# Second factor of a two-stage Fourier mixing: cosine and sine products in sixteen 32x32 tiles, two steps at a time

## The chip, the cores and the metric

The kernel runs on one core of a Trainium2 chip. The metric is the device time of one execution in microseconds (us). The median of three runs before the change is 2624.26 us (2623.59 to 2626.94).

## What is computed

Two blocks follow one another, all in fp32:

```python
# block 1: 8 sequences of 3008 rows, 256 channels; a filter in the frequency domain
X = np.fft.rfft(x, axis=1)                       # x: (8, 3008, 256)
Y = X * (filt_r + 1j * filt_i)[None, :, :]       # 1505 frequencies
y = np.fft.irfft(Y, n=3008, axis=1)
# block 2: every row through an ELU network
h = y.reshape(24064, 256) @ w_in                 # w_in: (256, 2048)
g = np.where(h > 0, h, np.exp(np.minimum(h, 0)) - 1)
out = g @ w_out                                  # w_out: (2048, 256)
```

## The kernel before, in words

**Block 1** is a Fourier transform in two factors, 3008 = 47 x 64. For each sequence ("batch" b) six `a_unit`s apply the factor of 64 and write to DRAM (`z_write`); eight steps g apply the factor of 47 and the filter (`b_unit`), four `bi_unit`s take the inverse factor of 47 (two steps at once) and write to DRAM (`y_write`), and six `n_unit`s (L438) take the inverse factor of 64. `b_unit` (L372) is what the change replaces. It has 16 matmuls whose weights are 48 rows by 32 columns: the 24 cosine and 24 sine rows of a table lie above each other, so that one matmul forms cosine product plus (or, for the other column half c, minus) sine product by itself. Real parts go to the PSUM tile `psr`, imaginary parts to `psi`. Then VectorE (DVE) multiplies both by the filter `f` (`products`, L328, four operations of 128x512 on a PSUM and an SBUF operand), and GpSimd (POOL) forms six sums in SBUF (L388 to L393; three small copies more in step 0).

**Block 2** takes the rows in 192 "items": 8 batches x 6 units m x 4 quarters q, each a multiplication by a quarter of `w_in` in Strassen-Winograd form: seven up steps (`up_steps`, L474; two matmuls each, for the trace four records, as each fp32 matmul is recorded twice), the ELU, and seven down steps by a quarter of `w_out` (`down_steps`, L559), one item later. In the prediction, U1 to U7 and D1 to D7 are these steps by the number of their product. The up steps run in the order U1 U2 U6 U5 U7 U3 U4, the down steps in the order D1 D3 D5 D7 D6 D2 D4. What matters of the up steps:

```python
def s2(): add("b11", mm(2, "a", True), g["t1"]); done("a")        # L517, DVE L497 from PSUM pha
def s7(): add("b22", mm(7, "d", True), g["t4"]); elu_max("b11", g["b11"])   # bank phd, DVE L497
def s3(): p = mm(3, "s", False); elu_exp("b12", p); ...; elu_max("b12", p); done("s")
def s4(): add("b21", mm(4, "d", False), g["t2"]); done("d"); elu_max("b22", g["b22"])
```

After U4, `tail` (L544) issues `elu_exp` of b21 and five DVE operations (L547, L548, L511, L550, L551). U4 accumulates into the same PSUM bank (`phd`) that U7 wrote, so its matmuls have to wait until DVE has read U7's result: the sum b22 of `s7`. `elu_exp` is two operations on ScalarE (ACT, L506 and L507), `elu_max` one on DVE (L511); `keep` (L500) is a copy by ACT.

**PSUM.** Four banks are dealt out in turn by the list `banks` (L187): each `bank()` takes the first, and its number is put back at the end of the list where the program is done with it. A `b_unit` takes two, a `bi_unit` all four.

**The order** is written by hand. The program runs over "quads", one per item (L903 to L922). In each quad the up steps of item i and the down steps of item i - 1 are interleaved by a string; between its first and second half come the planned units of place 0, at its end those of place 1:

```python
for k in "DUUDUDDU" if i in opens else "UUDUDDU": ...     # first half
for fn, a in plan.get((i, 0), ()): fn(*a)                 # place 0
for k in "DUUDUD" if i in opens else "DUUDUDD": ...       # second half
if up_tail: up_tail()
if down_tail: down_tail()
for fn, a in plan.get((i, 1), ()): fn(*a)                 # place 1
```

A quad in `opens` starts with a down step, which gives the banks time to come free. The plan repeats every 24 quads (one batch; "quad 10" below is the tenth of the 24). Seven batches have the steps of block 1 in it; the first has them ahead of the loop. Before, `b_unit`s stand at place 1 of quads 9, 10, 12, 13, 15, 16, 18, 19, `bi_unit`s at place 1 of 11, 14, 17, 20; quads 12, 15, 18, 21 open. Others in the plan: `x_unit` (L213, DVE), `c_unit` (four DVE sums, L587, place 0 of quads 1, 5, 9, 13, 17, 21), `o_unit` (two DVE transposes, L609, place 0 of 2, 6, 10, 14, 18, 22), three DVE sums of `down_steps`' tail (L587, at the end of quads 0, 4, 8, 12, 16, 20), `n_unit` and its three DVE sums `n_sums` (L458). Every engine takes its instructions in program order.

Of the kernel before, what the change touches and what calls it, by code (L numbers as in the profile page):

```python
# [14 lines left out]
ALU = mybir.AluOpType  # L15
# [26 lines left out]
def _make_tables():  # L42
# [58 lines left out]
    fb, bb = np.zeros((P, 2, 2, 32)), np.zeros((P, 2, 4, 32))  # L101
    for r in (LO, HI):
        fb[r, :, 0, :24] = gb[r, :, 0:24]
        fb[r, 0, 1, 1:24] = gb[r, 0, 24:47]
        fb[r, 1, 1, :24] = gb[r, 1, 24:48]
# [6 lines left out]
    pairs = np.concatenate([fb.reshape(P, P), bb.reshape(P, 2 * P)], 1)  # L112
# [18 lines left out]
def kernel(  # L131
# [27 lines left out]
    qp = pool("qp", 1)  # L159
    t3p = pool("t3p", 1)  # L160
# [8 lines left out]
    pairs = glob.tile([P, 3 * P], FP32, name="pairs")  # L169
    fb = pairs[:, 0:P].rearrange("p (v c k) -> p v c k", v=2, c=2)  # L170
    bb = pairs[:, P:3 * P].rearrange("p (v a i) -> p v a i", v=2, a=4)
# [71 lines left out]
    def x_place_first(c):  # L243
        if c < XBUFS:
            t = xp.tile([P, 2, 2, D], FP32, tag="xc", name="xc").rearrange("p k u d -> p (k u) d")
        else:
            t = t1p.tile([P, XC, D], FP32, tag="t1", name="x1")
        if c < 2:
            w = tnp.tile([P, 4, P], FP32, tag="tn", name="tn")
# [57 lines left out]
    def z_read(b, g):  # L307
        t = t2s[b, g] = t2p.tile([P, 4, D], FP32, tag="t2", name="t2")
        for p, r in enumerate((0, 24, 64, 88)):
            k = p * K2 + 4 * g  # L310
            nc.sync.dma_start(t[r:r + 24].rearrange("i u d -> i (u d)"), zs[b][:, k:k + 4, :].rearrange("i u d -> i (u d)"))
# [60 lines left out]
    def b_unit(b, g):  # L372
        t = t2s.pop((b, g))
        f = fbufs[(b * NG + g) % FBUFS]
        (i0, re), (i1, im) = (bank(n) for n in ("psr", "psi"))
        for c in range(2):
            for a in range(4):
                for ps, k in ((re, LO), (im, HI)):
                    nc.tensor.matmul(ps[32 * a:32 * a + 32, c, :], fb[k, 1 if g == a == 0 else 0, c, :], t[k, a, :],  # L379
                                     start=True, stop=True)  # L380
        sr, si = (sp.tile([P, 2, D], FP32, tag=n, name=n) for n in ("sr", "si"))
        if g % 2 == 0:
            ss[b, g] = qp.tile([P, 4, 2, D], FP32, tag="z", name="zs")
        z = ss[b, g - g % 2][:, :, g % 2]
        p, q = z[:, 0:2], z[:, 2:4]
        products(re, im, f, sr, si, p, q)
        banks.extend((i0, i1))
# [14 lines left out]
    def bi_unit(b, g):  # L402
        z = ss.pop((b, g))
# [302 lines left out]
    def f_arrange():  # L706

        for c, src in enumerate((filt_r, filt_i)):
            for a in range(2):
                nc.gpsimd.dma_start(fd[:, a, 0:48:2, c, :, :].rearrange("g q u d -> q g (u d)"),  # L710
                                    raw(src, 2 * a, [[64 * D, 24], [4 * D, NG], [1, 2 * D]]))
                for u in range(2):
                    g0 = 1 if a == u == 0 else 0
                    for j, n in ((0, 16), (16, 7)):
# [20 lines left out]
    with tc.manual_schedule():  # L735


        with tc.tile_pool(name="boot", bufs=1) as bp:
# [131 lines left out]
        for b in range(B):  # L870
            t = (b - 1) * PER
            if b > 0:
                for c, s in enumerate((2, 2, 4, 4, 7, 7)):
                    at(t + s, 0, x_unit, b, c)
                    if c % 2 == 0:
                        opens.add(t + s + 1)
                        at(t + s, 1, a_unit, b, c)
                    nb, nxt = (b, c + XBUFS) if c + XBUFS < NXC else (b + 1, c + XBUFS - NXC)
                    if nb < B:
                        at(t + s, 1, x_load, nb, nxt)  # L880
                    at(t + s, 1, z_write, b, c)
                for g in range(NG):
                    s = t + 9 + g + g // 2
                    at(s, 1, b_unit, b, g)
                    at(s - 2, 1, f_read, b, g)
                    at(s - 2, 1, z_read, b, g)
                    if g % 2:

                        opens.add(s + 2)
                        at(s + 1, 1, bi_unit, b, g - 1)  # L890
                        at(s + 1, 1, y_write, b, g - 1)
            for m, (s, place) in enumerate(((23, 0), (25, 1), (29, 1), (32, 0), (36, 0), (40, 0))):
                if b > 0 or m > 0:
# [4 lines left out]
                    at(*((t + s + 1, 1) if m == 5 else (t + s, place)), n_sums, b, m)  # L898
# [56 lines left out]
```

## Time and profile before

| | |
|---|---|
| median of three runs | 2624.26 us |
| the profiled execution, its own time | 2626.73 us |
| its span in the trace | 2624.9 us |
| busy: PE, DVE, ACT, POOL | 2556.2, 1891.1, 1483.2, 488.0 us |
| matmuls of b_unit (L379), psr and psi | 896 + 896 records, 376 ns each |
| DVE, L330 to L333 (products, 56 each) | 0.68 us each |
| POOL L388 | 56, mean 1.27 us |

PE is TensorE's matmuls. A row of the profile's groups reads: line, engine, operation, what is written <- what is read, shapes, count | busy time, mean of one | idle time of the engine just before it, and what ended that idle time. A row of the timeline reads: start, duration, engine, line, operation, operands, count. Successive operations of an engine overlap a little in the records (a DVE operation of 0.68 us is followed by the next one 0.60 us after its start), and full-array matmul records of 0.38 us start 0.216 us apart.

### The profile page before, as it was taken

To read this page: it belongs to the slowest core of one execution; us is meant where nothing else is said; L and a number is where in the kernel's file an instruction comes from. 1 tells how busy PE (TensorE), PEld (TensorE's weight loads), DVE (VectorE), ACT (ScalarE), POOL (GpSimd) and SP (SyncE) were. 2 spreads that over 40 slices of the span, in tenths; PEclk is the share of its full clock that TensorE was granted. 3 is DMA by queue.
4 is the path that set the end of the run, shared out by engine and by line. 5 is a ranking of instruction groups with operands and counts; after the bars stand their busy time and mean duration, and the time that the engine had idled before them with its cause. 6 is when DMAs were issued, how large, how long until landed. Compare 5 with 4: busy or idle time off the path is not lost.

```text
span 2624.9 us, 45659 instructions
## 1 busy us (share of the span) xinstructions
PE 2556.2 (97%) x17604; PEld 2173.1 (83%) x17604; DVE 1891.1 (72%) x3251; ACT 1483.2 (57%) x2574; POOL 488.0 (19%) x669
## 2 busy tenths in 40 slices
PE   5799999999999999999999999999999999999998
PEld 4588788888898888988889888888788888898887
DVE  6886777678777777777767777677777768766766
ACT  6565555555555555655555555555555555555554
POOL 5102330024200331004310133002340023300000
PEclk8899999999999999999999999999999999999999
DMA  9633221432224232232314231143321332210010
GB/s 275 185 102 101 72 61 36 121 87 59 67 66 113 61 87 48 66 102 66 88 41 102 73 99 48 41 106 87 91 56 40 84 82 63 61 37 18 19 27 17
DMA packets 227449, 200.50 MB, mean 76 GB/s; under 512 B 129554, under 2 KB 199410, under 8 KB 227232
## 3 DMA queue, kind: packets, MB, share of 16 engines
q1 hardware_dynamic: 209928, 160.60, 24.6%
q0 software_dynamic: 15856, 36.25, 4.9%
q8 instruction: 139, 2.28, 0.4%
q10 hardware_dynamic: 1448, 0.72, 0.1%
q14 instruction: 78, 0.64, 0.1%
HBM read 125.62 MB, written 78.17 MB: 78 GB/s over the span
## 4 chain that ended last, share of the span: by engine, by line
PE 91%; DVE 3%; ACT 2%; issue 0%; DMA 0%; SPq 0%; ACTq 0%; DVEq 0%
PE po L571 42%; PE phs L489 25%; PE phd L489 12%; PE pha L489 6%; PE psr L379 2%; PE psa L230 2%; PE pv L412 1%; DVE y L454 1%; PE psn L447 1%; DVE g L497 1%; ACT e L506 1%; ACT e L507 1%; ACT g L500 1%; ACT ys L452 0%; DVE ys L465 0%
## 5 line engine op out<-in xcount | busy, mean ns | idle before, releaser
L571 PE MATMUL po<-g,wo 128*128 128x256 f32 (+1 forms) x5376 | 1308.6, 376 | 0.0
L571 PEld LDWEIGHTS po<-g,wo 128*128 128x128 f32 x5376 | 1014.2, 190 | 142.7 <-issue 20.0
L500 ACT ACTIVATE g<-phs 128x512 f32<-128x512 f32 (+1 forms) x576 | 339.4, 589 | 827.6 <-PE phs L489 827.6
L497 DVE TENSOR_TENSOR g<-phd,g 128x512 f32<-128x512 f32 (+1 forms) x384 | 259.6, 676 | 376.9 <-ACT e L507 318.5
L507 ACT ACTIVATE e<-e 128x512 f32<-128x512 f32 (+1 forms) x768 | 477.4, 622 | 24.4
L511 DVE SCALAR_TENSOR_TENSOR g<-e,g 128x512 f32<-128x512 f32 (+1 forms) x576 | 400.5, 695 | 2.5 <-ACT e L507 1.3
L489 PE MATMUL phs<-y,wi 128*128 128x256 f32 (+1 forms) x1536 | 396.3, 380 | 1.4 <-DVE y L454 1.4
L489 PE MATMUL phs<-ys,wi 128*128 128x256 f32 (+1 forms) x1536 | 388.3, 375 | 1.5 <-ACT g L500 1.5
L506 ACT ACTIVATE e<-g 128x512 f32<-128x512 f32 (+1 forms) x576 | 353.7, 614 | 51.6 <-DVE g L511 24.3
L489 PEld LDWEIGHTS phs<-y,wi 128*128 128x128 f32 x1536 | 284.3, 190 | 58.1 <-issue 11.5
L489 PEld LDWEIGHTS phs<-ys,wi 128*128 128x128 f32 x1536 | 292.1, 190 | 35.6 <-ACT g L500 2.4
L388 POOL TENSOR_TENSOR sr<-sr,zs 128x512 f32<-128x512 f32 x56 | 71.3, 1273 | 1130.6 <-DVE zs L332 1130.6
L489 PE MATMUL phd<-ys,wi 128*128 128x256 f32 (+1 forms) x768 | 197.5, 380 | 16.4 <-DVE g L497 16.4
L511 DVE SCALAR_TENSOR_TENSOR g<-e,phs 128x512 f32<-128x512 f32 (+1 forms) x192 | 129.7, 675 | 110.4 <-ACT e L507 110.4
L506 ACT ACTIVATE e<-phs 128x512 f32<-128x512 f32 (+1 forms) x192 | 113.0, 589 | 146.8 <-PE phs L489 146.8
L489 PE MATMUL pha<-y,wi 128*128 128x256 f32 (+1 forms) x768 | 194.4, 376 | 0.0
L489 PE MATMUL phd<-y,wi 128*128 128x256 f32 (+1 forms) x768 | 193.7, 375 | 0.0
L489 PEld LDWEIGHTS phd<-ys,wi 128*128 128x128 f32 x768 | 142.8, 190 | 45.4 <-DVE g L497 30.5
L454 DVE SCALAR_TENSOR_TENSOR y<-ys,psn 128x512 f32<-128x512 f32 (+1 forms) x96 | 60.4, 671 | 148.5 <-ACT ys L452 148.5
L489 PEld LDWEIGHTS pha<-y,wi 128*128 128x128 f32 x768 | 146.4, 191 | 16.7
L489 PEld LDWEIGHTS phd<-y,wi 128*128 128x128 f32 x768 | 145.8, 190 | 16.5
L497 DVE TENSOR_TENSOR g<-pha,g 128x512 f32<-128x512 f32 (+1 forms) x192 | 129.1, 673 | 40.0 <-PE pha L489 40.0
(129 smaller groups left out, 2367.5 us busy)
## 6 DMA issues: line engine op xcount, KB each, us to landing
t<-yd SPq DMA_DIRECT2D x95, 256.0 KB
z<-t SPq DMA_DIRECT2D x84, 256.0 KB
f<-fp POOLq DMA_DIRECT2D x224, 96.0 KB, 3.0
t<-z SPq DMA_DIRECT2D x224, 96.0 KB
yd<-t SPq DMA_DIRECT2D x112, 192.0 KB
out_dram<-o SPq DMA_DIRECT2D x632, 32.0 KB
xc<-in_x_dram SPq DMA_DIRECT2D x84, 128.0 KB
xc<-in_x_dram SPq DMA_DIRECT2D x161, 64.0 KB
```

The lines of the kernel that those rows point to most:

```text
L230: nc.tensor.matmul(p[o:o + 64, u, :], w[r, u, o:o + 64], src[r, u, :], start=True, stop=True)
L379: nc.tensor.matmul(ps[32 * a:32 * a + 32, c, :], fb[k, 1 if g == a == 0 else 0, c, :], t[k, a, :], start=True, stop=True)
L388: nc.gpsimd.tensor_tensor(out=sr, in0=sr, in1=p, op=ALU.add)
L412: nc.tensor.matmul(pv[a][1][32 * p:32 * p + 32, js, :], bb[r, v, p, :], z[r, p, js, :], start=True, stop=True, tile_position=(32 * a, 32 * p))
L454: nc.vector.scalar_tensor_tensor(out=y, in0=s[:, 0:2], scalar=v, in1=even[:, :, 0:h], op0=ALU.mult, op1=ALU.add)
L489: nc.tensor.matmul(ps[:, a, 0:h], w_in[q][:, COMBO[n], a, :], y[n], start=start and a == 0, stop=True, skip_group_check=True)
L497: nc.vector.tensor_tensor(out=g[o], in0=i0, in1=i1, op=ALU.add)
L500: nc.scalar.activation(out=g[o], in_=i0, func=AXT.Copy)
L506: nc.scalar.activation(out=e, in_=src, func=AXT.Relu, scale=-1.0)
L507: nc.scalar.activation(out=e, in_=e, func=AXT.Exp, scale=-1.0)
L511: nc.vector.scalar_tensor_tensor(out=g[n], in0=es[n], scalar=1.0, in1=src, op0=ALU.subtract, op1=ALU.max)
L571: nc.tensor.matmul(po[i][:, u, 0:h], w_out[q][:, COMBO[n], a, :], g[n][:, a, :], start=q == 0 and a == 0 and n in (1, 3, 6, 4), stop=True, ...
```

## The change

`b_unit` is split into `b_pair` (two steps g and g + 1 at once) and `b_products` (one step).

`b_pair` has 32 matmuls with weights of 24 rows by 32 columns: cosine and sine products are apart, each in one of four row groups (`tile_position`), and go to four PSUM banks (xr, yr, yi, xi). ACT copies yr and yi to SBUF; DVE then forms sum and difference of x and y for real and imaginary parts (four operations of 128x512), into the SBUF tiles `s` (a new pool) and `z`; in step 0 four copies of 32x256 follow. `b_products` multiplies as before, but reads SBUF alone and works in place; then POOL does what it did. `b_pair` and the products of the even step stand at place 1 of quads 9, 12, 15, 18, the products of the odd step at place 0 of the next quad; `bi_unit` stays where it was. Quads 10, 13, 16 and 19 open now, besides 12, 15, 18, 21. Reads of the filter and of z for both steps are issued together, two quads ahead of `b_pair`. `n_unit` of m = 4 moves from place 0 of quad 12 to place 0 of 14, that of m = 5 from place 0 to place 1 of 16, and every `n_sums` half a quad later. The table `fb` is cut to 64 columns, the padding of the filter is written as zeros, and some tiles of the start come from other pools.

```diff
+    for p, (r, c) in enumerate(((0, 0), (24, 24), (64, 24), (88, 0))):
+        fb[32 * p:32 * p + 24, 0, :24] = gb[r:r + 24, 0, 0:24]
+        fb[32 * p:32 * p + 24, 1, :24] = gb[r:r + 24, 1, c:c + 24]
...
-        for p, r in enumerate((0, 24, 64, 88)):
+        for p in range(4):
             k = p * K2 + 4 * g
-            nc.sync.dma_start(t[r:r + 24].rearrange("i u d -> i (u d)"), zs[b][:, k:k + 4, :].rearrange("i u d -> i (u d)"))
+            nc.sync.dma_start(t[32 * p:32 * p + 24].rearrange("i u d -> i (u d)"), zs[b][:, k:k + 4, :].rearrange("i u d -> i (u d)"))
...
-    def b_unit(b, g):
-        t = t2s.pop((b, g))
+    def b_pair(b, g):
+        t = [t2s.pop((b, g + j)) for j in range(2)]
+        pb = [bank("psb") for _ in range(4)]
+        for j in range(2):
+            for a in range(4):
+                for p, (_, ps) in enumerate(pb):
+                    r = slice(32 * p, 32 * p + 24)
+                    nc.tensor.matmul(ps[32 * a:32 * a + 32, j, :], fb[r, 1 if g == j == a == 0 else 0, :], t[j][r, a, :],
+                                     start=True, stop=True, tile_position=(32 * p, 32 * a))
+        s = rp.tile([P, 2, 2, D], FP32, tag="s", name="s")
+        z = qp.tile([P, 4, 2, D], FP32, tag="z", name="zs")
+        ss[b, g] = s, z
+        xr, yr, yi, xi = (ps for _, ps in pb)
+        ur, ui = (sp.tile([P, 2, D], FP32, tag=n, name=n) for n in ("sr", "si"))
+        nc.scalar.activation(out=ur, in_=yr, func=AXT.Copy)
+        nc.scalar.activation(out=ui, in_=yi, func=AXT.Copy)
+        for o, x, u in ((s, xr, ur), (z, xi, ui)):
+            nc.vector.tensor_tensor(out=o[:, 0], in0=x, in1=u, op=ALU.add)
+            nc.vector.tensor_tensor(out=o[:, 1], in0=x, in1=u, op=ALU.subtract)
+        if g == 0:
+            for o, x, u in ((s, xr, ur), (z, xi, ui)):
+                nc.vector.tensor_copy(out=o[0:32, 0, 0], in_=x[0:32, 0])
+                nc.vector.tensor_copy(out=o[0:32, 1, 0], in_=u[0:32, 0])
+        banks.extend(pb[p][0] for p in (1, 2, 0, 3))
+
+    def b_products(b, g):
         f = fbufs[(b * NG + g) % FBUFS]
-        (i0, re), (i1, im) = (bank(n) for n in ("psr", "psi"))
-        for c in range(2):
-            for a in range(4):
-                for ps, k in ((re, LO), (im, HI)):
-                    nc.tensor.matmul(ps[32 * a:32 * a + 32, c, :], fb[k, 1 if g == a == 0 else 0, c, :], t[k, a, :],
-                                     start=True, stop=True)
...
-        products(re, im, f, sr, si, p, q)
-        banks.extend((i0, i1))
+        s, z = ss[b, g - g % 2]
+        sr, p, q = s[:, :, g % 2], z[:, 0:2, g % 2], z[:, 2:4, g % 2]
+        n = "sr" if g % 2 else "si"
+        si = sp.tile([P, 2, D], FP32, tag=n, name=n)
+        nc.vector.tensor_tensor(out=si, in0=sr, in1=f[:, 1], op=ALU.mult)
+        nc.vector.tensor_tensor(out=sr, in0=sr, in1=f[:, 0], op=ALU.mult)
+        nc.vector.tensor_tensor(out=q, in0=p, in1=f[:, 0], op=ALU.mult)
+        nc.vector.scalar_tensor_tensor(out=p, in0=p, scalar=-1.0, in1=f[:, 1], op0=ALU.mult, op1=ALU.mult)
         nc.gpsimd.tensor_tensor(out=sr, in0=sr, in1=p, op=ALU.add)
...
-                for g in range(NG):
+                for g in range(0, NG, 2):
                     s = t + 9 + g + g // 2
-                    at(s, 1, b_unit, b, g)
-                    at(s - 2, 1, f_read, b, g)
-                    at(s - 2, 1, z_read, b, g)
-                    if g % 2:
-                        opens.add(s + 2)
-                        at(s + 1, 1, bi_unit, b, g - 1)
-                        at(s + 1, 1, y_write, b, g - 1)
-            for m, (s, place) in enumerate(((23, 0), (25, 1), (29, 1), (32, 0), (36, 0), (40, 0))):
+                    opens.update((s + 1, s + 3))
+                    at(s, 1, b_pair, b, g)
+                    for j in range(2):
+                        at(s - 2, 1, f_read, b, g + j)
+                        at(s - 2, 1, z_read, b, g + j)
+                        at(s + j, 1 - j, b_products, b, g + j)
+                    at(s + 2, 1, bi_unit, b, g)
+                    at(s + 2, 1, y_write, b, g)
+            for m, (s, place) in enumerate(((23, 0), (25, 1), (29, 1), (32, 0), (38, 0), (40, 1))):
...
-                    at(*((t + s + 1, 1) if m == 5 else (t + s, place)), n_sums, b, m)
+                    at(t + s + place, 1 - place, n_sums, b, m)
```

More of the change, by code (lines that the diff above doesn't have):

```diff
@@ L97, in _make_tables @@
     gi[0:24, 1, 24:48], gi[24:48, 1, 0:24] = -m0 * s0.T, -m3 * s3.T
[L101 to L105, printed above, removed]
+    fb, bb = np.zeros((P, 2, 32)), np.zeros((P, 2, 4, 32))
+    for p, (r, c) in enumerate(((0, 0), (24, 24), (64, 24), (88, 0))):
+        fb[32 * p:32 * p + 24, 0, :24] = gb[r:r + 24, 0, 0:24]
+        fb[32 * p:32 * p + 24, 1, :24] = gb[r:r + 24, 1, c:c + 24]
     for o in range(0, P, 32):
@@ L111, in _make_tables @@
     bb[0:24, 1, 2, :24], bb[0:24, 1, 3, :24] = gi[24:48, 1, 0:24], gi[0:24, 1, 24:48]
-    pairs = np.concatenate([fb.reshape(P, P), bb.reshape(P, 2 * P)], 1)
+    pairs = np.concatenate([fb.reshape(P, 64), bb.reshape(P, 2 * P)], 1)
     lie = np.concatenate([2 * np.arange(24), 2 * np.arange(24) + 1])
@@ L146 @@
     ]
+    none_d = nc.inline_tensor(np.zeros((NG, 2 * D), np.float32), name="none_t").ap()
     def pool(name, bufs, **kw):
@@ L159 @@
     qp = pool("qp", 1)
+    rp = pool("rp", 1)
     t3p = pool("t3p", 1)
@@ L167 @@
     psM = pool("psM", 1, space=PSUM)
-    pairs = glob.tile([P, 3 * P], FP32, name="pairs")
-    fb = pairs[:, 0:P].rearrange("p (v c k) -> p v c k", v=2, c=2)
-    bb = pairs[:, P:3 * P].rearrange("p (v a i) -> p v a i", v=2, a=4)
+    pairs = glob.tile([P, 64 + 2 * P], FP32, name="pairs")
+    fb = pairs[:, 0:64].rearrange("p (v k) -> p v k", v=2)
+    bb = pairs[:, 64:].rearrange("p (v a i) -> p v a i", v=2, a=4)
     w_in, w_out = ([glob.tile([P, 7, 2, P], FP32, name="%s%d" % (n, i)) for i in range(4)] for n in ("wi", "wo"))
@@ L248, in x_place_first @@
         if c < 2:
-            w = tnp.tile([P, 4, P], FP32, tag="tn", name="tn")
+            w = sp.tile([P, 4, P], FP32, tag="s" + "ri"[c], name="tf")
         else:
@@ L367, in y_write_first @@
             queues[p // 2].dma_start(yds[0][32 * p + 4 * g:32 * p + 4 * g + 4].rearrange("u i d -> i u d"), t[r:r + 24])
-    def b_unit(b, g):
-        t = t2s.pop((b, g))
-        f = fbufs[(b * NG + g) % FBUFS]
-        (i0, re), (i1, im) = (bank(n) for n in ("psr", "psi"))
-        for c in range(2):
-            for a in range(4):
-                for ps, k in ((re, LO), (im, HI)):
-                    nc.tensor.matmul(ps[32 * a:32 * a + 32, c, :], fb[k, 1 if g == a == 0 else 0, c, :], t[k, a, :],
-                                     start=True, stop=True)
[L381 to L385, printed above, removed]
-        products(re, im, f, sr, si, p, q)
-        banks.extend((i0, i1))
+    def b_pair(b, g):
[22 more added lines that the diff above has]
+        banks.extend(pb[p][0] for p in (1, 2, 0, 3))
@@ L402, in bi_unit @@
     def bi_unit(b, g):
-        z = ss.pop((b, g))
+        _, z = ss.pop((b, g))
         t = t3s[b, g] = t3p.tile([P, 2, 4, D], FP32, tag="t3", name="t3")
@@ L719, in f_arrange @@
                 g0 = 0 if a else 1
-                nc.gpsimd.dma_start(fd[g0:NG, a, 47, c, :, :].rearrange("g u d -> g (u d)"),
-                                    raw(src, 4, [[2 * D, NG - g0], [1, 2 * D]]))
+                nc.gpsimd.dma_start(fd[g0:NG, a, 47, c, :, :].rearrange("g u d -> g (u d)"), none_d[g0:NG])
             nc.gpsimd.dma_start(fd[0, 0, 1:48:2, c, 0, :], raw(src, 32, [[64 * D, 24], [1, D]]))
-            nc.gpsimd.dma_start(fd[0, 0, 47:48, c, 1, :], raw(src, 4, [[D, 1], [1, D]]))
+            nc.gpsimd.dma_start(fd[0, 0, 47:48, c, 1, :], none_d[0:1, 0:D])
     def f_pairs(c, u):
@@ L744 @@
             zq = qp.tile([P, 4, 2, D], FP32, tag="z", name="zq")
-            pqs = [[(sp if i == 0 else bp).tile([P, 2, D], FP32, name="s%s" % n, **({"tag": "s" + n} if i == 0 else {}))
-                    for n in "ri"] +
-                   [zq[:, 0:2, i], zq[:, 2:4, i]] for i in range(2)]
             t3f = t3p.tile([P, 2, 4, D], FP32, tag="t3", name="t3")
@@ L807 @@
             w_join(6)
+            pqs = [[(sp if i == 0 else bp).tile([P, 2, D], FP32, name="s%s" % n, **({"tag": "s" + n} if i == 0 else {}))
+                    for n in "ri"] +
+                   [zq[:, 0:2, i], zq[:, 2:4, i]] for i in range(2)]
             for g in range(4):
```

## The prediction

> **What bounds the kernel now.** I read the page's busy times and the chain that ended last, then PE's list of waits, then the timeline around one batch's steps.
>
> ```profile
> PE 2556.2 (97%) x17604; PEld 2173.1 (83%) x17604; DVE 1891.1 (72%) x3251; ACT 1483.2 (57%) x2574; POOL 488.0 (19%) x669
> ...
> PE 91%; DVE 3%; ACT 2%; issue 0%; DMA 0%; SPq 0%; ACTq 0%; DVEq 0%
> ```
>
> PE is the bound: it idles 69 us, most of it in the first 120 us. PE's time is what counts, and whatever makes PE wait. In the loop only one wait recurs:
>
> ```profile
> PE phd L489 <- DVE g L497: 16.4, 29, 0.7
> ```
>
> This is U4 waiting for DVE's sum b22 (front section). U7's end leaves DVE two steps of PE, 1.73 us, to do it. The timeline shows it at 1163.66 in quad 8, behind the `n_unit`'s five DVE operations, and U4 0.66 us late. So DVE has 28% to spare on average and none at this place: what is queued ahead of b22 shows as a stall of PE. The change queues more there.
>
> **PE's saving.** The unit of 16 matmuls (32 records) before: the D step ahead of it starts at 1260.01, its last record is at 1260.66; the unit's records run from 1260.97 to 1261.69; U1 starts at 1261.99, with its second record 0.32 later instead of 0.216. Added to PE: 1261.99 - 1260.66 - 0.216 = 1.117, plus 0.104 = 1.22 us. For sixteen tiles of 32x32 the nearest row is `bi_unit`:
>
> ```profile
> 1011.69 0.59 PE L571 MATMUL po<-g,wo 128*128 128x256 f32 x2
> 1012.22 1.14 PE L412 MATMUL pv<-zs,pairs 24*32 24x512 f32 x32
> 1013.29 0.70 PE L571 MATMUL po<-g,wo 128*128 128x256 f32 x2
> ```
>
> Its 32 records are twice as wide as b_pair's and need 1.07 us to the next step, two rounds of sixteen, 0.45 us apart; sixteen tiles do run at once. b_pair has four rounds of 256 columns: 0.31 (lead) + 0.77 (0.24 + 2 x 0.215 to the fourth round, then 15 issues at 0.0067) + 0.31 - 0.216 + 0.104 = 1.27 us. A pair saves 2 x 1.22 - 1.27 = 1.17 us, 28 pairs **-32.7 us**. If only eight tiles ran at once, it were four more rounds of 0.215, and -8.6 us in all.
>
> **What DVE gets.** Let T be b_pair's first record. The records of b_pair end 0.77 after T, D1 starts at 1.08; in an opening quad twelve steps of 0.864 us stand ahead of U4, so U4 is due at 1.08 + 0.10 + 12 x 0.864 = T + 11.55. Ahead of b22, the program order of the changed kernel has on DVE: the last quad's tail, b_pair's four sums, the even step's four products, b11, the planned units of place 0, the odd step's four products. Row L330 to L333 prices them: started 0.60 us apart (1225.60, 1226.19, 1226.79, 1227.39), 0.68 long. An operation that writes in place what the one before it reads starts 0.72 after it (L547 at 1261.59, L548 at 1262.30); two of four products do, so 2.64 us for four. SBUF-only operands cost the same 0.68 (L550).
>
> The tail ends at T + 3.0 in quad 10 (L330 at 1181.42, T at 1178.41). After an opening quad it is T + 3.87 (1264.84, 1260.97). There b_pair also waits for b21's read of bank phd, which two-bank units did not: 0.16 us of PE, three times a batch, +3.4 us in all; the tail then ends at T + 3.7.
>
> Quads 16 and 19: 3.7 + 2.4 + 2.64 + 0.6 = 9.34 to the odd products, + 2.64 = 11.98, b22 done 12.66, U4 at 12.72: **1.2 us late, with nothing going wrong**. Quad 10: from 3.0, with four copies of 32x256 (not in the trace; 0.35 each as the 128x256 rows, from 0 to 0.6, so 0 to 2.4 together) and two transposes (1.24): 3.1 late. Quad 13: three tail sums (1.0) and `c_unit` (1.46): 3.6 late. Together 9.1 us a batch, 64 us in seven; from these rows alone the saving is spent twice. Behind the waiting U4 stand D4 and the whole next quad on PE; DVE's b21 waits for U4 in turn, and in quads 11, 14 and 20 DVE catches up (by the same reckoning b22 is 0.4 early in 14, where `n_unit` 4 now stands).
>
> **What POOL adds.** The odd products now run while POOL forms the even step's sums, and both read only SBUF. Before, products read PSUM and POOL started after them. The trace shows what happens when such operations meet, first on DVE, then on POOL:
>
> ```profile
> 1228.59 0.52 DVE L587 TENSOR_TENSOR k<-k,c 128x256 f32<-128x256 f32 x1
> 1229.14 0.83 DVE L587 TENSOR_TENSOR c<-c,k 128x256 f32<-128x256 f32 x1
> 1229.90 0.41 DVE L587 TENSOR_TENSOR c<-po,k 128x256 f32<-128x256 f32 x1
> 1230.23 0.61 DVE L587 TENSOR_TENSOR c<-k,k 128x256 f32<-128x256 f32 x1
> 1230.77 0.68 DVE L497 TENSOR_TENSOR g<-phd,g 128x512 f32<-128x512 f32 x1
> 1231.37 1.17 DVE L511 SCALAR_TENSOR_TENSOR g<-e,g 128x512 f32<-128x512 f32 x1
> ```
>
> ```profile
> 1227.56 1.27 POOL L388 TENSOR_TENSOR sr<-sr,zs 128x512 f32<-128x512 f32 x1 [20.89 <-DVE zs L332]
> 1228.90 0.79 POOL L389 TENSOR_TENSOR zs<-sr 128x256 f32<-128x256 f32 x1
> 1229.66 0.91 POOL L390 TENSOR_TENSOR zs<-sr 128x256 f32<-128x256 f32 x1
> 1230.53 1.46 POOL L391 TENSOR_TENSOR si<-si,zs 128x512 f32<-128x512 f32 x1
> 1232.06 1.06 POOL L392 TENSOR_TENSOR zs<-si 128x256 f32<-128x256 f32 x1
> ```
>
> Operations with one operand in PSUM (L497, c<-po,k) keep their time. Those with two in SBUF end a fixed time after POOL's operation: L511 at 1232.53, 0.55 after L391's end (1231.98); 0.28 for 256 columns. POOL's next one ends 0.60 after DVE's (L392), 1.14 if 512 wide. They take turns. [...]
>
> With turns in quads 16 and 19: the even products end at 8.82, L388 runs 8.96 to 10.24; odd products end at 10.79, 11.94, 13.09 and, after POOL's wide sum, 14.78; b22 15.38; U4 at 15.45, 3.9 late. Likewise quad 10 (the first odd product meets L389): 5.4; quad 13 (`c_unit` takes turns too): 7.1. Together 20.3 a batch, **+142 us**. Without turns it is 64. One of the four products follows an independent one 0.60 later and might keep its turn: then about 1 us less each, 114.
>
> **The clock.** Stalls of 4 us are new. Stretches of 3.41 us from the start of the trace (span, busy PE, PEld, DVE, ACT, POOL, then PE's granted clock):
>
> ```profile
> 40.00:43.41 3.41, 1.46 (x13) 1.30 (x12) 3.27 (x7) 3.14 (x8) 0.00 (x0) 0.99 1.05 366
> 43.41:46.82 3.41, 3.06 (x16) 2.67 (x16) 2.79 (x7) 1.74 (x5) 2.84 (x6) 0.51 0.97 289
> 46.82:50.24 3.42, 3.42 (x36) 3.13 (x36) 0.44 (x2) 3.27 (x8) 1.30 (x3) 0.99 1.06 209
> ```
>
> After a stretch with PE idle for 1.95 us the next has half the clock; after one with 0.35 idle it is full. A stretch at half clock does 1.7 us less work. A stall of 3.9 us or more leaves some stretch at least half idle. I charge one half-clock stretch per stall: 4 x 1.7 x 7 = **+48 us** (bounds 0, where the half-clock stretch passes within the stall, and twice that). [...]
>
> **The rest.** Quad 17 starts with DVE late and has `c_unit` and now three `n_sums` ahead of b22: 2.75 late with turns, less 1.7 where the clock slows PE: +7 us in all (0 to 19). `n_sums` out of the way: U4 on time in quads 8 and 12, eight times 2 x 0.66: -10.6; in quad 23 it gains 0.56, but now its sums come after the tail, and U6 of quad 0, due 2.4 after that quad's start, needs the second: done 3.9 after, 1.5 late: net +0.95 x 7 = +6.7. ACT's two copies (0.60 each) stand ahead of U1's result, and U1's bank is free when it comes. POOL (7 us a step) is done 4 us ahead of `bi_unit`; reads of f (3.0 us to landing; eight issues of 0.50 on POOL, now behind a pair's sums instead of a step's) and z are issued two quads, 24 us, ahead, z_read of the odd step past one quad's SP work; z and t2 buffers are free by then. The reads for `n_unit` 4 move with it on SP, still two quads ahead. Zeros for padding replace equal DMAs. These I cost at nothing; if POOL were late, a few tenths in quad 11.
>
> **Sum:** -32.7 + 3.4 + 142 + 48 + 7 - 3.9 = +164 on the profiled execution's 2626.7: 2790.5; the median lies 2.5 under it: **2788 us**.
>
> **Rivals and chances.** What a measurement tells from no change is about 0.2%, 5 us.
> - Forecast, turns and slow clock, 0.5: 2788; its own range 2740 (clock 0) to 2815 (clock more, quad 17 in full).
> - Turns in part, with one product per pair unblocked, 0.2: 2788 - 28 = 2760.
> - No turns, the plain queue, 0.2: 64 of stalls, a half-clock stretch in some of quads 10 and 13 (17): -32.7 + 3.4 + 64 + 17 - 3.9 = +48, 2672; without clock 2655. For it: tail operations beside POOL (L550) keep 0.68; but there POOL only issues DMAs.
> - **Faster**, 0.06: b22 in time in every quad, so that PE's saving stands: -32.7 - 3.9: 2588. It decides where DVE's queue ahead of b22 is under T + 11.5, that is 0.5 us or less per operation, or where U4 doesn't wait; break-even is 5.2 us of stall a batch. Against it: 0.60 in every row, and the 0.66 us at quad 8.
> - Eight tiles at once instead of sixteen: +24 on any of these, 0.02.
>
> Faster 0.06, same 0.02 (stalls of just the break-even size, the last of the chances), slower 0.92. The range 2655 to 2815 takes in the first three.
>
> **What would show it.** PE's waits phd <- DVE L519 (L497 before) near 145 us in 28 large places, longest in quad 13; L406 to L409 of odd steps over 1 us each, those of even steps 0.68; POOL's mean over 1.3; PEclk digits of 8 and 9 mixed in the middle slices; the small-tile unit at 1.27 us. Wrong: if phd's waits stay near 16 us, or the odd products take 0.68.

## The result and the profile after

The changed kernel takes 2794.64 us (median of four runs, 2791.80 to 2796.07) against 2623.93 us for the kernel before on the same chip (four runs, 2623.32 to 2626.94): ratio **1.0647 [1.0634, 1.0661]**, 6.5% slower. The span grew by 165.1 us, from 2624.9 to 2790.0. The forecast was 2788 us with a range of 2655 to 2815.

Here is the page of the changed kernel: the busy times, the granted clock in 40 slices, and the shares of the chain that ended last.

```profile
PE 2596.6 (93%) x17604; PEld 2214.5 (79%) x17604; DVE 2107.0 (76%) x3391; ACT 1518.1 (54%) x2630; POOL 561.4 (20%) x669
...
PEclk8899999999999999999999999999999999999999
...
PE 75%; DVE 18%; issue 3%; ACT 2%; DMA 2%; DVEq 0%; SPq 0%; ACTq 0%
```

PE's share fell from 97% to 93% although its busy time rose by 40 us. DVE's busy time rose by 216 us and POOL's by 73, while the sums that were added (four of 0.68 us a pair and a few copies) come to no more than 84 us: DVE is busy for longer with work that it had before. In the chain, DVE has 18% where it had 3%. The clock's digits are too coarse to show anything: the mean granted clock fell from 0.992 to 0.963, which stays inside a digit of 9.

PE's list of waits in the changed kernel (total us, times, longest):

```profile
PE phd L511 <- DVE g L519: 136.5, 37, 6.7
...
PE phs L511 <- DVE ys L486: 9.8, 7, 1.4
```

The first row is U4 waiting for b22, 16.4 us before. Nearly all of it lies at four places of every batch: quads 10, 13, 16 and 19 cost 4.62, 6.65, 3.47 and 3.47 us, each seven times (127 us), and quad 17 costs 2.27 us in three batches (7 us) and 0.09 in the others. The second row is new: U6 in quad 0, behind the sums of `n_unit` 0 that come half a quad later now.

Three timelines of the same stretch, the odd step's products in quad 16 of one batch, show how one such wait comes about. First DVE in the changed kernel (start, duration, operation):

```profile
1350.75 1.38 DVE L406 TENSOR_TENSOR sr<-s,f 128x512 f32<-128x512 f32 x1
1352.17 1.10 DVE L407 TENSOR_TENSOR s<-s,f 128x512 f32<-128x512 f32 x1
1353.19 1.21 DVE L408 TENSOR_TENSOR zs<-zs,f 128x512 f32<-128x512 f32 x1
1354.44 1.64 DVE L409 SCALAR_TENSOR_TENSOR zs<-zs,f 128x512 f32<-128x512 f32 x1
1355.99 0.68 DVE L519 TENSOR_TENSOR g<-phd,g 128x512 f32<-128x512 f32 x1
```

Then POOL, which forms the even step's sums meanwhile:

```profile
1351.67 1.05 POOL L411 TENSOR_TENSOR zs<-s 128x256 f32<-128x256 f32 x1
1352.68 1.17 POOL L412 TENSOR_TENSOR zs<-s 128x256 f32<-128x256 f32 x1
1353.81 1.71 POOL L413 TENSOR_TENSOR si<-si,zs 128x512 f32<-128x512 f32 x1
```

And PE, with its idle time and the releaser in brackets:

```profile
1352.23 1.03 PE L593 MATMUL po<-g,wo 128*128 128x256 f32 x4
1356.73 1.13 PE L511 MATMUL phd<-ys,wi 128*128 128x256 f32 x4 [3.46 <-DVE g L519]
```

Add up starts and durations. L406 ends at 1352.13, POOL's L411 at 1352.72, DVE's L407 at 1353.27, POOL's L412 at 1353.85, DVE's L408 at 1354.40, POOL's L413 at 1355.52, DVE's L409 at 1356.08. The two engines' ends alternate without exception here; DVE's come 0.54 to 0.56 us after POOL's, POOL's 0.58 to 0.59 (256 wide) or 1.12 (512 wide) after DVE's. The four products take 5.3 us where 2.6 were the price without POOL. b22 itself (L519), with one operand in PSUM, keeps its 0.68 us, and U4 starts 0.06 us after its end.

The half clock has its place in the timeline and the stretches too. Around the wait of quad 13 in another batch PE shows:

```profile
969.08 2.08 PE L511 MATMUL phd<-ys,wi 128*128 128x256 f32 x4 [6.65 <-DVE g L519]
970.95 1.91 PE L593 MATMUL po<-g,wo 128*128 128x256 f32 x4
972.66 1.18 PE L511 MATMUL phs<-y,wi 128*128 128x256 f32 x4
```

The first two steps after the wait take 2.08 and 1.91 us for what takes 1.13 and 1.03 elsewhere. Stretches of 3.41 us around this wait, and around the wait of 3.46 us above (span, then busy PE, PEld, DVE, ACT, POOL, then the granted clock):

```profile
962.42:965.84 3.42, 0.01 (x1) 0.00 (x0) 3.38 (x5) 1.03 (x2) 3.34 (x4) 1.00 0.00 0
965.84:969.25 3.41, 0.17 (x1) 0.17 (x2) 3.38 (x5) 0.00 (x0) 2.06 (x3) 0.54 0.00 0
969.25:972.66 3.41, 3.41 (x9) 2.70 (x9) 3.13 (x4) 1.97 (x4) 3.33 (x4) 0.50 0.00 0
972.66:976.08 3.42, 3.42 (x17) 3.03 (x16) 3.38 (x4) 1.15 (x2) 3.34 (x6) 0.96 0.00 0
1351.54:1354.95 3.41, 1.72 (x8) 1.16 (x7) 3.34 (x4) 1.85 (x3) 3.33 (x4) 1.00 0.00 0
1354.95:1358.36 3.41, 1.63 (x8) 1.44 (x8) 3.38 (x5) 1.02 (x2) 3.33 (x4) 1.00 0.00 0
```

The long wait leaves a whole stretch of PE empty, and the next ones run near 0.50. The wait of 3.46 us falls across two stretches, leaves each of them about half busy (1.72 and 1.63 us), and the clock stays at 1.00. The 0.54 and the 0.96 say that these stretches start some 0.3 us ahead of the clock's own changes, which the trace has at 966.13 and 972.96. With stretches that start on those changes, the long wait empties the one from 962.72 to 966.13, and the short one leaves 1.42 us busy from 1351.84 and 1.93 us from 1355.25. PE's busy time at half clock, times the half that is lost, comes to 2.3 us in the loop before and 62.0 after (worked out from the changes of the clock and PE's records).

**The account.** Worked out from the starts and ends of PE's records in the loop: waits +129.9 us (the two rows above), lost clock +59.7, the small-tile units -20.9; the start-up ahead of the loop came out 5.8 shorter, but it varies by that much between traces in which nothing of it was changed (97.3 to 103.7 us). These make +162.9 of the +165.1 us, and the other 2 stay open. A wait also costs a little more than it lasts: the first step after it is recorded longer (1.13 us instead of 1.03), and quad 8, where a wait of 0.66 is gone, became 0.93 shorter.

### The profile page after: what moved, and what is told of

It is laid out like the page before. It is cut to its first block, busy times and chain, and to the rows that moved or that the text cites. A ratio compares the mean times of both kernels' runs of the same rounds, so it can differ in the third digit from the quotient of the medians.

```text
span 2790.0 us, 45790 instructions
## 1 busy us (share of the span) xinstructions
PE 2596.6 (93%) x17604; PEld 2214.5 (79%) x17604; DVE 2107.0 (76%) x3391; ACT 1518.1 (54%) x2630; POOL 561.4 (20%) x669
## 4 chain that ended last, share of the span: by engine, by line
PE 75%; DVE 18%; issue 3%; ACT 2%; DMA 2%; DVEq 0%; SPq 0%; ACTq 0%
PE po L593 34%; PE phs L511 20%; PE phd L511 11%; PE pha L511 5%; DVE g L519 2%; DVE g L533 2%; DVE zs L408 2%; PE psn L469 2%; DVE s L407 2%; PE psa L232 1%; DVE sr L406 1%; PE pv L434 1%; DVE g L570 1%; DVE g L569 1%; DVE g L572 1%
## 5 line engine op out<-in xcount | busy, mean ns | idle before, releaser
L593 PE MATMUL po<-g,wo 128*128 128x256 f32 (+1 forms) x5376 | 1340.5, 382 | 0.0
L593 PEld LDWEIGHTS po<-g,wo 128*128 128x128 f32 x5376 | 1029.4, 193 | 160.0 <-issue 31.6
L519 DVE TENSOR_TENSOR g<-phd,g 128x512 f32<-128x512 f32 (+1 forms) x384 | 259.6, 676 | 376.9 <-ACT e L529 298.6
L533 DVE SCALAR_TENSOR_TENSOR g<-e,g 128x512 f32<-128x512 f32 (+1 forms) x576 | 423.9, 736 | 0.9 <-ACT e L529 0.2
L511 PE MATMUL phd<-ys,wi 128*128 128x256 f32 (+1 forms) x768 | 217.5, 409 | 136.9 <-DVE g L519 136.5
L511 PEld LDWEIGHTS phs<-y,wi 128*128 128x128 f32 x1536 | 297.6, 196 | 42.6 <-ACT t L437 3.2
L410 POOL TENSOR_TENSOR s<-s,zs 128x512 f32<-128x512 f32 x56 | 71.0, 1268 | 1192.8 <-DVE zs L409 1192.8
L511 PEld LDWEIGHTS phd<-ys,wi 128*128 128x128 f32 x768 | 151.7, 203 | 170.2 <-DVE g L519 153.3
L519 DVE TENSOR_TENSOR g<-pha,g 128x512 f32<-128x512 f32 (+1 forms) x192 | 129.4, 674 | 44.6 <-PE pha L511 44.3
L570 DVE TENSOR_TENSOR g<-g,g 128x512 f32<-128x512 f32 (+1 forms) x192 | 146.5, 763 | 6.7
```

The source lines that it names most:

```text
L410: nc.gpsimd.tensor_tensor(out=sr, in0=sr, in1=p, op=ALU.add)
L511: nc.tensor.matmul(ps[:, a, 0:h], w_in[q][:, COMBO[n], a, :], y[n], start=start and a == 0, stop=True, skip_group_check=True)
L519: nc.vector.tensor_tensor(out=g[o], in0=i0, in1=i1, op=ALU.add)
L533: nc.vector.scalar_tensor_tensor(out=g[n], in0=es[n], scalar=1.0, in1=src, op0=ALU.subtract, op1=ALU.max)
L570: nc.vector.tensor_tensor(out=b12, in0=b22, in1=b12, op=ALU.subtract)
L593: nc.tensor.matmul(po[i][:, u, 0:h], w_out[q][:, COMBO[n], a, :], g[n][:, a, :], start=q == 0 and a == 0 and n in (1, 3, 6, 4), stop=True, ...
```

## The experiments

My theory: (1) DVE has no room ahead of b22 in quads 10, 13, 16 and 19, so that eight more operations make U4 late even at their bare price; (2) the turns with POOL double what the odd products cost; (3) the clock adds nearly half of the waits on top; PE's saving is lost in these waits. The rivals that the runs are to tell apart: it is only the *place* of the odd products that costs, and PE's saving can be had at another place; POOL's sums cost what they cost, wherever they lie; PE's own unit, slower than predicted, is to blame. Each run is set beside runs of the kernel before, whose medians lay between 2623.15 and 2625.29 us.

### POOL's sums left out

```diff
-        nc.gpsimd.tensor_tensor(out=sr, in0=sr, in1=p, op=ALU.add)
...
-                nc.gpsimd.tensor_copy(out=q[0:32, i], in_=si[0:32, 1 - i])
```

> The changed kernel with POOL's sums of the products left out (bi_unit takes the products as they are). Theory (turns of DVE and POOL lengthen the odd products): L406 to L409 of odd steps take 0.69 like those of even steps, the stalls at U4 fall to 2.6, 3.2, 0.8, 0.8 us in quads 10, 13, 16, 19 and vanish in 17, 52 us in all instead of 134, and half clock falls from 52 us over the full rate to 25 to 40: 2672 us, 2650 to 2690. Rival (the plain queue on DVE is nearly all of it): above 2740.

Measured: 2675.33 us (one run). One product's line, first in the changed kernel, then in this one (count, then shortest, median and longest in ns):

```profile
L408 DVE TENSOR_TENSOR zs<-zs,f x56: 684/946/1746, 229.6 to 2424.3; 128x512 f32<-128x512 f32 x56
```

```profile
L408 DVE TENSOR_TENSOR zs<-zs,f x56: 682/684/687, 233.3 to 2311.6; 128x512 f32<-128x512 f32 x56
```

The longest of 56 is now 0.687 us, with 1.746 in the changed kernel: the whole lengthening goes with POOL's sums. PE's first wait of this kernel:

```profile
PE phd L499 <- DVE g L507: 54.6, 34, 3.3
```

The waits of U4 are 2.36, 3.35, 0.89 and 0.89 us in quads 10, 13, 16 and 19, and none in 17. They stand for point (1): without any turn the added DVE work is still too late. The difference to the full change, 119 us of time and 82 us of this wait, is point (2) with the clock that follows it (lost clock 24.0 us in the loop instead of 62.0).

### POOL's sums behind both steps' products

```diff
+        pend.append((si, q))
+        if g % 2 == 0:
+            return
+        nc.gpsimd.tensor_tensor(out=s, in0=s, in1=z[:, 0:2], op=ALU.add)
...
```

> The changed kernel with all its work, but POOL's first sum is taken over both steps at once, so that POOL starts only after the odd products. Theory: odd products at 0.69, stalls at U4 as without POOL (2.6, 3.2, 0.8, 0.8), but POOL's 11 us then run beside the tail of DVE and the next quad: up to 2 us more in quad 17 and some of the maxima at over 1 us: 2680 us, 2660 to 2715. Rival: the turns cost the same wherever they fall, and the time stays above 2760; or bi_unit waits for POOL in quads 11, 14, 17, 20 and shows as waits pv <- POOL.

Measured: 2781.87 us (one run), a miss by 100 us: the rival that I had named beside it won. The products are as short as without POOL. A line of the even and odd products in this kernel:

```profile
L409 DVE TENSOR_TENSOR s<-s,f x56: 691/691/693, 233.2 to 2414.8; 128x512 f32<-128x512 f32 x56
```

The waits in quads 10, 13, 16 and 19 are down to 2.36, 3.35, 0.89 and 0.89 us, as without POOL. But the list of waits says:

```profile
PE phd L517 <- DVE g L525: 103.5, 68, 3.7
...
PE po L599 <- DVE c L615: 9.8, 7, 1.4
```

68 waits instead of 37. POOL now starts behind the odd products, beside b22, and meets what DVE does next, the quad's tail, whose operations read only SBUF as well. DVE's timeline where POOL starts, in this kernel (POOL's sum of 128x1024 runs there from 1350.04 for 2.35 us):

```profile
1349.87 0.68 DVE L525 TENSOR_TENSOR g<-phd,g 128x512 f32<-128x512 f32 x1
1350.47 2.46 DVE L539 SCALAR_TENSOR_TENSOR g<-e,g 128x512 f32<-128x512 f32 x1
```

L525 reads PSUM and is undisturbed; L539 ends at 1352.93, 0.54 us after POOL's 1352.39. Over all 576 of this operation the mean, in the groups of the kernel before and of this one, is:

```profile
L511 DVE SCALAR_TENSOR_TENSOR g<-e,g 128x512 f32<-128x512 f32 (+1 forms) x576 | 400.5, 695 | 2.5 <-ACT e L507 1.3
```

```profile
L539 DVE SCALAR_TENSOR_TENSOR g<-e,g 128x512 f32<-128x512 f32 (+1 forms) x576 | 476.7, 828 | 15.8 <-ACT e L535 15.3
```

76 us more for this one line, and the waits come back one quad later: 0.6 to 2.1 us in quad 11, 0.9 to 3.1 in 14, 3.7 and then 1.4 (of a down step, the second row above) in 17, 0.8 and 0.7 in 20 (with the waits for ACT that stand beside them in 11, 14 and 20). So the turns' price is paid where POOL's sums meet DVE's SBUF-only operations: here at L539 (up to 2.53 us), in the changed kernel at the odd products too (up to 1.75 us).

### Odd products at the end of the quad

```diff
-                        at(s + j, 1 - j, b_products, b, g + j)
+                        at(s + j, 1, b_products, b, g + j)
```

> The changed kernel with the odd step's four products at place 1 of quads 10, 13, 16, 19 instead of place 0, so that they no longer stand ahead of b22 on DVE. Theory (time is lost where U4 waits for b22): PE's waits phd <- DVE fall from 136.5 us to 15 to 25 (about 2 us are left in quad 13, where c_unit meets POOL), the 50 us of half clock go with them: 2625 us, 2612 to 2640. Rival A (it is DVE's whole load, not the place): the lag moves to the next quad and the time stays above 2720. Rival B: POOL, now done later, makes bi_unit wait in quads 11, 14, 17, 20, 2 us or more each: above 2680.

Measured: 2714.77 us (2714.09 to 2715.91), ratio 1.0346 [1.0331, 1.0362]. Half of the loss is gone, but 2625 was expected. PE's wait for b22:

```profile
PE phd L511 <- DVE g L519: 64.3, 31, 6.2
```

There is none left in quads 10, 16 and 19, and 2.0 in 13, as reckoned. What was overlooked is quad 17, now 6.14 us: the last operation of `n_unit` 5, its sums, the odd products of 16 and `c_unit` all stand ahead of its b22. The second part is `bi_unit`, which the rival in the expectation had named: the odd step's sums on POOL are late for it. PE at the end of quad 11:

```profile
1241.13 1.47 PE L434 MATMUL pv<-zs,pairs 24*32 24x256 f32 x20
1242.82 2.18 PE L434 MATMUL pv<-zs,pairs 24*32 24x512 f32 x20 [0.22 <-POOL zs L414]
```

From its first to its last record a `bi_unit` takes 3.28 us here and 2.66 in quad 20, where the others take 0.92 and 0.55: 4.5 us more a batch, 31 us in seven. The list of waits shows only 0.2 of it a time, because the matmuls wait in turn for one tile after the other and the records overlap: in quad 11 POOL's last two sums end at 1242.76 and 1243.89, and the next matmuls start at 1242.82 and 1243.94. Against the change the loop is 82 us shorter: 70 us of PE's idle time and 40 of lost clock are gone, and these 31 have come.

### Matmuls of 512 columns

```diff
-        for j in range(2):
-            for a in range(4):
-                for p, (_, ps) in enumerate(pb):
...
+        for a, p, js, v in both:
+            r = slice(32 * p, 32 * p + 24)
+            nc.tensor.matmul(pb[p][1][32 * a:32 * a + 32, js, :], fb[r, v, :], t[r, js, a, :],
```

> The changed kernel with both steps of a pair in one matmul of 512 columns (32 records instead of 64, one weight load for both steps). Theory: the unit takes 1.16 us instead of 1.6, like bi_unit, but in quads 10, 13, 16, 19 DVE sets when U4 starts, counted from the unit's start, so the stalls grow by the same 0.43 us each and the time stays: 2795 us, 2785 to 2800. Rival (PE's own time counts as before): 12 us less, 2783 or lower.

Measured: 2796.61 us (2793.28 to 2797.51), ratio 1.0655 [1.0637, 1.0673]. Two steps side by side in one tile halve the number of matmuls, and the unit adds 1.41 us to PE instead of 1.72 (worked out from the records as below). The time is the same as that of the change, and PE's wait takes the gain up:

```profile
PE phd L514 <- DVE g L522: 138.4, 41, 6.9
```

The four waits are 4.84, 6.94, 3.76 and 3.76 us, each 0.2 to 0.3 longer, 7.6 us in seven batches of the 7.9 that the unit gained (0.20 us in a batch's first pair, 0.31 in the others). U4 is due earlier and b22 is done when it was: which shows that PE's own work no longer sets the end at these places. The row grew by only 1.9 us, as quad 17's wait is under 0.3 us in all seven batches; but quad 16 ran at half clock in all seven instead of four, and the lost clock is 67.3 us instead of 62.0.

### Sums of n_unit 0 back ahead of quad 23's end

```diff
-                    at(t + s + place, 1 - place, n_sums, b, m)
+                    at(t + s + place, 1 - place if m else 0, n_sums, b, m)
```

> The changed kernel with n_sums of m = 0 alone back in the middle of quad 23. Theory: U6 of quad 0 no longer waits 1.4 us for the second sum (quad 0 from 12.97 to 11.34 us), U4 of quad 23 waits 0.4 again (13.35 to 14.02): -11.4 + 4.7 = -6.7 us, 2788 us. Rival: no difference.

Measured: 2790.23 us (2789.48 to 2791.59), ratio 1.0636 [1.062, 1.0652], 4.4 us under the change. Quad 0 went from 12.97 to 11.34 us, quad 23 from 13.35 to 14.02 (distances of first records, worked out from the trace). The row of U6's wait is gone. So both places moved as reckoned, by -6.7 us together; but quad 16 ran at half clock in all seven batches here (18.7 us each), the lost clock grew from 62.0 to 74.8 us, and quad 17's wait of 2.27 us in three batches is gone in return. The loop of the profiled execution is only 1.3 us shorter.

### Three edits together, with n_unit 4 and 5 back

Odd products at the end of the quad, matmuls of 512 columns, and the units and sums that crowded quads 13, 14 and 17 at other places:

```diff
-                        at(s + j, 1 - j, b_products, b, g + j)
+                        at(s + j, 1, b_products, b, g + j)
...
-            for m, (s, place) in enumerate(((23, 0), (25, 1), (29, 1), (32, 0), (38, 0), (40, 1))):
+            for m, (s, place) in enumerate(((23, 0), (25, 1), (29, 1), (32, 0), (36, 0), (40, 0))):
...
```

> The changed kernel with odd products at place 1, matmuls of 512 columns, n_unit of m = 4 and 5 back at place 0 of quads 12 and 16, n_sums of m = 0, 1, 2, 3, 4, 5 at 23 middle, 2 middle, 6 middle, 8 end, 14 middle, 17 end. Theory: now PE's saved time counts (1.07 + 0.10 us a pair, 33 us), and stalls are left in quad 13 (2.4, c_unit in turns with POOL), 23 and 2 (0.4 each) and a few tenths in 10 and 11: 24 us against 18 before: 2600 us, 2590 to 2615. Rival (DVE's added 84 us of work, not its place, costs time): above 2624.

Measured: 2693.80 us (2691.46 to 2697.40), ratio 1.0269 [1.0254, 1.0284]. Better than the first two edits alone (2714.77 and 2796.61; the third was not run alone), far from 2600, and the theory that only these places cost falls with it. The rival's time came, but that DVE's added work by itself is the cause is not shown by it.

```profile
PE phd L514 <- DVE g L522: 59.4, 48, 2.9
```

The waits are spread: 2.28 us in quad 13, 1.18 to 2.87 in 14, 2.55 in 17, 0.4 in 11 and 16. `bi_unit` is still 3.28 us long in quad 11 and 2.55 in quad 20, some 30 us in seven batches. With 46 us more of PE's idle time than in the kernel before, 24 more of lost clock and 29 less for the units that is 71 of the 74 us by which the loop is longer; so a large part of what is left stands at `bi_unit`, behind POOL. One more step in the same direction moved two `c_unit`s half a quad ahead:

```diff
-                at(t + PER + 4 * m + 5, 0, c_unit, b, m)
+                at(t + PER + 4 * m + (4 if m in (2, 3) else 5), 1 if m in (2, 3) else 0, c_unit, b, m)
```

> As e7_combined, with c_unit of the units that fall into quads 13 and 17 one place earlier, ahead of b_pair's sums on DVE, when POOL is idle. Theory (turns): the four sums take 1.46 us instead of 2.9, quad 13's stall falls from 2.4 to 1.0: 10 us less than e7_combined, 2590 us. Rival (length of DVE's queue alone): the same work stands ahead of b22, so the time is that of e7_combined within 3 us.

Measured: 2705.75 us (2704.23 to 2707.94), ratio 1.0314 [1.0299, 1.0329]: slower than without it.

```profile
PE phd L514 <- DVE g L522: 52.9, 48, 3.9
...
PE pv L437 <- POOL zs L417: 2.8, 14, 0.2
```

Quad 13 fell from 2.28 to 0.97 us and quad 17 from 2.55 to 1.24, as expected; quad 14 rose to 3.88, and `bi_unit` waits for POOL twice a batch instead of once: that of quad 17 takes 3.28 us instead of 0.55, 19 us in seven batches, more than the 12 by which the time grew. Each move made its own place better and another one worse.

### Places in the kernel before

If the sums' places are worth something by themselves, they must be worth it in the kernel before. First two of its `n_sums` half a quad later:

```diff
-                    at(*((t + s + 1, 1) if m == 5 else (t + s, place)), n_sums, b, m)
+                    at(*((t + s + 1, 1) if m == 5 else (t + s, 1 if m in (3, 4) else place)), n_sums, b, m)
```

> The kernel before with one part of the change alone: n_sums of m = 3 and 4 at the end of quads 8 and 12 instead of in the middle. Theory (what stands ahead of b22 costs PE): U4's 0.66 us waits in quads 8 and 12 vanish, and with the slow start after each wait these quads shrink by 0.93, as quad 8 did in the changed kernel (13.44 to 12.51): 16 x 0.93 = 15 us less, 2609 us (2605 to 2613). Rival (the sums only move the wait to quads 9 and 13): 2624.

Measured: 2615.39 us (seven runs, 2613.15 to 2619.17), ratio 0.997 [0.9959, 0.9982], between the two forecasts.

```profile
PE phd L489 <- DVE g L497: 12.8, 20, 1.0
```

Quads 8 and 12 each became 0.93 us shorter, but 13 got a wait of 1.0 that it had not had, so that half of the gain moved on. With the places chosen by this, sums of m = 3 to place 1 of quad 8 as here, sums of m = 4 two quads after their `n_unit` and the `o_unit` of m = 5 a quad later:

```diff
-                    at(*((t + s + 1, 1) if m == 5 else (t + s, place)), n_sums, b, m)
+                    at(t + ((23, 0), (25, 1), (29, 1), (32, 1), (38, 0), (41, 1))[m][0], ((23, 0), (25, 1), (29, 1), (32, 1), (38, 0), (41, 1))[m][1], n_sums, b, m)
...
-                at(t + PER + 4 * m + 6, 0, o_unit, b, m)
+                at(t + PER + 4 * m + (7 if m == 5 else 6), 0, o_unit, b, m)
```

> The kernel before with three places moved and none of the new work: n_sums of m = 3 at the end of quad 8, of m = 4 in the middle of quad 14, o_unit of m = 5 in the middle of quad 3 instead of 2. Theory (only what stands ahead of b22 counts): U4's waits vanish in quads 8, 12 and 2 and none comes in 13, where the sums at the end of 12 had cost 1.0: 16 x 0.93 + 6 x 0.7 = 19 us less than before, 2605 us (2600 to 2611). Rival (waits move on): no faster than the 2615 us of the kernel with the two sums alone moved.

Measured: 2605.89 us (2600.94 to 2607.01), ratio 0.993 [0.9917, 0.9944]. This kernel leaves out the last batch's last `o_unit`, as its move takes it past the end; with that unit at its old place (`7 if m == 5 and b < B - 1 else 6`):

> As e10_before_places, which left out the last o_unit (two transposes and 32 writes to the output at the very end); here it stays where it was, so that all work is done. Theory: U4's waits are gone as there, and the end costs what it did before: 2608 us (2603 to 2613). Rival: no faster than the 2615 us of the kernel with two sums moved.

Measured: **2611.82 us** (2609.06 to 2612.42), ratio **0.9951 [0.9937, 0.9964]**: the fastest kernel of the study that does the whole computation, 13 us under the one before. Its wait for b22, and its busy times:

```profile
PE phd L489 <- DVE g L497: 7.2, 14, 0.6
```

```profile
PE 2549.0 (98%) x17604; PEld 2174.8 (83%) x17604; DVE 1899.2 (73%) x3251; ACT 1482.4 (57%) x2574; POOL 487.9 (19%) x669
```

DVE's busy time is not less than before. Only the order changed, and 9 us of waits went with it. Not all are gone: quad 23 kept its 0.4 us, and quad 14 got 0.62 that it had not had.

## Why the prediction was right, and what was mis-sized

**The bound.** It was read from a single row: U4 waits 0.66 us in quad 8, so DVE has no room ahead of b22. That row carried the whole forecast; the average of 28% to spare would have led to the faster case.

**PE's saving** was the mis-sized term. Predicted: 1.27 us a pair, -32.7 us by 28 pairs. PE in the changed kernel around one `b_pair`:

```profile
949.75 0.59 PE L593 MATMUL po<-g,wo 128*128 128x256 f32 x2
950.28 1.60 PE L381 MATMUL psb<-t,pairs 24*32 24x256 f32 x64
951.80 1.13 PE L593 MATMUL po<-g,wo 128*128 128x256 f32 x4
```

The first matmul record after a unit starts 0.31 us after the unit's last one, the unit 0.31 after the record ahead of it (here 949.97), as before. From first to last record the unit takes 1.22 us (1.12 in a batch's first pair), where the working had 0.77. By that reckoning it adds 1.72 us to PE (1.62 in the first), and two units of 1.22 less that make 20.9 us over 28 pairs instead of 32.7. The failed step is "2 x 0.215 to the fourth round, then 15 issues at 0.0067". The records' starts in a batch's first pair show where: the first 32 come as assumed, 0.0067 us apart, the second sixteen 0.24 after the first; the 34th comes at 0.650 instead of some 0.46, and from there on most follow 0.0167 us apart, so that sixteen take some 0.25. In the other pairs the first 32 come in bursts, with the 32nd at 0.47, and the 34th again at 0.65. The row that I took, `bi_unit`, ends after 32 records (0.55 us from first to last) and can't show it. Why the pace changes there was not tried. Sixteen tiles do run at once in the first 32 (in a batch's first pair sixteen records of 0.37 us start within 0.10 us), so the rival with eight (0.02) is out. The 0.16 us for bank phd did not come: the unit starts 0.31 after the step ahead of it as ever.

**DVE's queue.** Predicted waits in quads 10, 13, 16, 19: 5.4, 7.1, 3.9, 3.9. Measured: 4.62, 6.65, 3.47, 3.47. Each is lower by 0.43 to 0.78, and 0.45 of that is the longer unit (1.72 against 1.27; in quad 10, behind the first pair, 0.35), behind which U4 is due later. The matmuls of 512 columns bear this out: with the unit 0.20 shorter ahead of quad 10 and 0.31 ahead of the others, the waits were 0.22 and 0.29 longer. Without turns: predicted 3.1, 3.6, 1.2, 1.2, measured 2.36, 3.35, 0.89, 0.89 in the run without POOL's sums. In total +127 us where +142 stood.

**The turns.** Right in place and size: the odd products' ends were predicted from two rows of the tail before. Wrong was the reservation behind the 0.2 rival: in quads 10, 16 and 19 all four products lose their turn, the independent one too, in every batch. In quad 13 three do; the fourth comes when POOL is done and takes 0.69 us. L408 takes 0.684 us beside an idle POOL and up to 1.746 beside a busy one. In quad 16's timelines each of the operations that meet is recorded as started before the other engine's ends, and ends 0.54 to 1.12 us after it.

**The clock.** +48 predicted, +59.7 measured, and not by the rule I charged. Not one stretch for each wait: behind quad 13's wait two stretches run at half clock (966.13 to 972.96), and quad 16's of 3.47 us costs either nothing or 2.57 us. Quad 16 is 18.71 us long in four batches and 16.14 in three (first records), by how its wait falls against the stretches of 3.41 us. In the traces of the kernel before and of the changed one all changes of the clock lie whole multiples of 3.413 us apart. In the stretch quoted in the prediction PE was busy for 1.46 of 3.41 us, and the next one had half the clock. In the changed kernel's loop, of the stretches at full clock that start on the clock's own changes, those with PE busy for 1.35 us or less were followed by half the clock, those with 1.42 or more by the full one (1.25 to 1.31 in quad 16 of the four batches, 1.42 in the three). With the odd products at the end of the quad one stretch of 1.42 us kept it and one lost it. In the start-up, stretches with up to 2.1 us busy lost it too, so the limit of some 1.4 us is shown for this loop alone. The bounds (0 to 96) held.

**Quad 17.** Predicted 1.0 net, and 2.75 where the clock does not slow PE. Measured: 2.27 in exactly the three batches in which quad 16 kept its full clock, 0.09 in the other four: 7.2 us against 7. (The three `n_sums` ahead of its b22 are those of m = 5: they stand half a quad earlier than before, not later as the section on the change has it for all.)

**The sums' places.** Quad 8 -0.93 and quad 23 -0.67 as expected in sign; U6 in quad 0 waits 1.4 us (predicted 1.5). By the waits alone the places come to -4.4 us against a predicted -3.9: U4 -10.6 in quads 8 and 12 and -3.6 in 23 and 2, U6 +9.8.

**The sum.** PE's gain was put too large by 12 us and the clock too small by 12; against that the waits in the four quads were put too large by 15, and the 3 for bank phd did not come. That these nearly cancel, so that 2788 lies 7 us from 2794.6, is luck; that the turns and the clock would carry the loss is not. **What would show it**: the waits at 136.5 (near 145 said), longest in quad 13, the odd products at 1 us or more (but for the last one of quad 13) and the even ones at 0.69 all came. L413 has a mean of 1.62 us where 1.32 stood (over 1.3 said, a weak test, as the mean before was at it already). PEclk digits of 8 among the 9s did not come: that view is too coarse for 3% of clock. The unit at 1.27 us was wrong.

**What stays open.** Whether a still better order gives PE's 20 us back was not settled: the best of the changed kernel's orders tried is 2693.8. That no order can is argued, not shown; the runs show that five of them do not. Doing the sums on ACT or leaving one operand in PSUM for the products, which might take the turns away at the root (operations with an operand there kept 0.69 us or less beside POOL's sums), was not tried.

## What to carry to other kernels

A change that saves the busiest engine time by giving another engine work is priced at the place where the first already waits for the second: here one wait of 0.66 us told more than 28% of idle time. Before putting VectorE work that reads only SBUF beside GpSimd work that reads SBUF, look in a trace at what such a meeting costs (here 1.0 to 1.75 us instead of 0.69 for 105 of 112 odd products) and at what is queued behind it. Where TensorE gets waits of several us, look at its clock behind them too: here 130 us of added waits came with 60 us of lost clock.

## What the runs showed of the hardware beyond expectation

- VectorE and GpSimd alternated, operation by operation, where a VectorE operation with two SBUF operands met GpSimd's sums: in the stretch of quad 16 the ends come 0.54 to 0.56 us (DVE, 512 columns) and 0.58 (POOL, 256) or 1.12 us (POOL, 512) after the other's end. In the changed kernel's loop all 272 such operations of 512 columns that overlap one of POOL's sums end 0.55 to 0.62 us after one ends; the 105 with an operand in PSUM that overlap one keep 0.69 us or less. Beside a POOL sum of 128x1024 one DVE operation took 2.46 us instead of 0.68.
- fp32 matmuls of 256 columns in sixteen tiles of 24x32, 64 records in a row: in a batch's first pair they start 0.0067 us apart within each of the first two rounds of sixteen and mostly 0.0167 us apart in the second half. With 512 columns and half as many matmuls the unit adds 0.20 us less in a batch's first pair and 0.31 in the others.
- In the changed kernel's loop a stretch of 3.413 us with TensorE busy for 1.42 us or more kept the full clock, one with 1.35 or less was followed by half the clock. So quad 16's wait of 3.46 us costs no clock at one phase and makes the quad 2.57 us longer at another (18.71 against 16.14).
